# Gated linear attention followed by a multiplicative feed-forward block: loads of a step in the order alpha, k and q, v, and the logarithm tied behind the transposed copies

## The chip, the cores and the metric

The kernel runs on one core of a Trainium2 chip. The metric is the device time of one execution in microseconds (us), smaller is better. Three timed runs of the kernel before the change took 478.72, 480.35 and 480.21 us; their median is 480.21 us.

## The reference

Inputs are `q`, `k`, `v` and `alpha`, each of shape batch 4, heads 8, sequence 768, head dimension 48 in fp32, and four weight matrices of the second block in float64. The first block is a recurrence with a decay per key channel, the second a feed-forward block with a product of two projections:

```
for t in range(768):                         # per batch and head
    state = alpha[t][:, None] * state + outer(k[t], v[t])      # 48 x 48
    y[t] = q[t] @ state
x = y, heads side by side                    # 3072 tokens x 384
a, b = x @ w1, x @ w2                        # 384 -> 1024 each
out = ((a * b) @ w3) @ w_out                 # 1024 -> 1024 -> 384
```

## The kernel before, in words

**Two parts.** Part 1 runs the recurrence in chunks of 128 positions. There are 6 chunks per batch, so N = 24 chunks, numbered 0 to 23 through all batches, and it is one loop over steps n = 0 to 24 that is written out at build time. Beside the attention, part 1 converts the float64 weights `w1` and `w2` into split fp32 ([...]`to_fp32` rebuilds each number from the two words of `raw`) and, from step 6 on, fills in products of the second block (`gate`, whose matrix products all stand on the helper line L420). Part 2 does the rest of the products, folds `w3` with `w_out`, and projects.

**One chunk through part 1.** For chunk m: `load_a`, `load_kq` and `load_v` (L132, L138 and L139, L144) bring alpha, k, q and v, each 192 KB in runs of 192 bytes. `logs(m)` takes the logarithm of alpha on ScalarE (L271, called Ln(m) below), for chunks from 10 on it also splits it into two parts (L275 on ScalarE, L276 on VectorE), and for some even chunks GpSimd copies one row of alpha out to DRAM (L278). `decays(m)` sums the logarithms along the chunk on TensorE (L286 for chunks before 10, L289 from 10 on), and ScalarE takes two exponentials (L292, L293). `decayed(m)` multiplies k and q with them on VectorE (L302). `transposed(m)` transposes the result on TensorE (L324), and ScalarE copies it out of PSUM in two instructions (L326); the second copy is `mark["qkT", m]`. `scores(m)` multiplies k and q (L364) and masks on VectorE (L367); `attend_state` (L384) and `attend` (L390, copied by L394) give y; `outer` (L336) advances the state.

**What a step calls.** Step n calls, in this order of the source: the stores of y of step n-1 (L261), the load of a group of x if one is due, `load_v(n + 3)`, `load_a(n + 5)`, `load_kq(n + 4)`, `attend_state(n - 1)`, `scores(n)`, `transposed(n + 1)`, some weight conversion, `attend(n - 1)`, `outer(n)`, a product of the conversion (`third`, L232 to L234), fill pieces, `decayed(n + 2)`, `logs(n + 4)`, and `decays(n + 3)`. So alpha of a chunk is first needed one step after the step that loads it, k and q two steps after, and v three steps after. Weight conversion issues its own loads (`raw`, L192, 512 KB each) on the same queue.

**What orders the work.** All these loads are issued by SyncE (SP) in one queue. The order in which each engine and queue gets its instructions is fixed when the program is built: the Tile framework goes by the order of the source as a priority and by its own estimate of when each operand is there, and puts an instruction with a late operand behind others that come later in the source. `issue_after(ins)` (used through `after_marks`) adds an edge to that ordering: what the block traces on the engine of `ins` is placed behind `ins` on that engine. Work of the block on other engines gets no such edge.

**Buffers.** `ac` (alpha) and `kq` have three buffers, v has five, `raw` four, `la` two, `la2` one. A load into `ac` waits for the logarithm of the chunk three before and for its row copy, a load into `kq` for L302 of the chunk three before, a load into v for L390 of the chunk five before.

Of the kernel before, what the change touches and what calls it, by code (L numbers as in the profile page):

```python
# [48 lines left out]
def kernel(  # L49
# [18 lines left out]
    N = B * NCH  # L68
# [8 lines left out]
    AHEAD = 4  # L77
# [30 lines left out]
    def after_marks(*names):  # L108
        stack = ExitStack()
        for x in names:  # L110
            stack.enter_context(tc.issue_after(mark[x]))
        return stack
# [12 lines left out]
    def rows(src, n):  # L125
        b, c = divmod(n, NCH)
        return src[b, :, ds(c * C, C), :].rearrange("h p d -> p h d")

    def load_a(n):
        if n < N:  # L130
            st["a", n] = inp.tile([C, H, D], FP32, tag="ac", name="ac")
            nc.sync.dma_start(out=st["a", n], in_=rows(alpha, n))  # L132

    def load_kq(n):
        if n >= N:
            return
        st["kq", n] = inp.tile([C, 2, H, D], FP32, tag="kq", name="kq")
        nc.sync.dma_start(out=st["kq", n][:, 0], in_=rows(k, n))  # L138
        nc.sync.dma_start(out=st["kq", n][:, 1], in_=rows(q, n))  # L139

    def load_v(n):
        if n < N:
            st["v", n] = vs[n % len(vs)]
            nc.sync.dma_start(out=st["v", n][:, :, 0:D], in_=rows(v, n))  # L144
# [91 lines left out]
    def fetch(ahead=3):  # L236
        while weights and len(begun) < ahead:
            begun.append(weights.popleft())
            next(begun[-1])

    def convert(steps, ahead=3):

        for _ in range(steps):
            fetch(ahead)
            if not begun:
                return
            x = begun.popleft()
            try:
                next(x)
                begun.appendleft(x)  # L250
            except StopIteration:
                pass
# [4 lines left out]
    def store():  # L257

        while later:
            dst, src = later.popleft()  # L260
            nc.sync.dma_start(out=dst, in_=src)  # L261
# [4 lines left out]
    def logs(n):  # L266
        if n >= N:
            return
        a = st.pop(("a", n)).rearrange("p h d -> p (h d)")
        la = st["la", n] = work.tile([C, DM], FP32, tag="la", name="la")  # L270
        nc.scalar.activation(la, a, AF.Ln)  # L271
        if n >= LATE:

            t = st["la", n] = work.tile([C, 2, DM], FP32R, tag="la2", name="la2", bufs=1)
            nc.scalar.copy(t[:, 0], la)  # L275
            nc.vector.tensor_sub(t[:, 1], la, t[:, 0].bitcast(FP32))  # L276
        if n in ends:
            nc.gpsimd.dma_start(out=ends[n][2:3], in_=a[0:1])  # L278

    def decays(n):  # L280
        if n >= N:
            return
        lc = bank()[:, 0:DM]
        la = st.pop(("la", n))
        if n < LATE:
            nc.tensor.matmul(lc, sums[:, n % 2].bitcast(FP32), la, start=True, stop=True)  # L286
        else:
            for i in range(2):
                nc.tensor.matmul(lc, sums[:, n % 2], la[:, i], start=(i == 0), stop=(i == 1))  # L289

        e = st["e", n] = work.tile([C, 2, DM], FP32, tag="e", name="e", bufs=3)
        nc.scalar.activation(e[:, 0], lc, AF.Exp, scale=-1.0)  # L292
        mark["e", n] = nc.scalar.activation(e[:, 1], lc, AF.Exp).ins  # L293
        if n in ends:
            nc.gpsimd.dma_start(out=ends[n][0:1], in_=e[0:1, 0])
        if n + 1 in ends:
            nc.gpsimd.dma_start(out=ends[n + 1][1:2], in_=e[C - 1:C, 1])
        load_ends(n)

    def decayed(n):  # L300
        if n < N:
            mark["qk", n] = nc.vector.tensor_mul(qks[n % 3][:, :, :, 0:D], st.pop(("kq", n)),  # L302
                                 st.pop(("e", n)).rearrange("p i (h d) -> p i h d", h=H)).ins
# [9 lines left out]
    def transposed(n):  # L313
        if n >= N:
            return
        qk = qks[n % 3]
        qkT = work.tile([C, 2, NP, C], FP32, tag="qkT", name="qkT")

        tp = [bank().rearrange("p (i j c) -> p i j c", i=2, j=NP) for _ in range(2)]
        for i in range(2):  # L320
            for j in range(NP):
                for half in range(2):
                    s = ds(DP * half, DP)
                    nc.tensor.transpose(tp[half][:, i, j, :], qk[s, i, 2 * j:2 * j + 2, :], ident[s, s])  # L324
        for half in range(2):
            mark["qkT", n] = nc.scalar.copy(qkT[:, :, :, ds(DP * half, DP)], tp[half]).ins  # L326
        st["qkT", n] = qkT
# [30 lines left out]
    def scores(n):  # L358
        qkT = st["qkT", n]
        sc = [bank().rearrange("p (j c) -> p j c", j=NP) for _ in range(2)]  # L360
        for j in range(NP):
            for i in range(2):
                r = ds(DP * i, D)
                nc.tensor.matmul(sc[i][:, j, :], qkT[r, 0, j, :], qkT[r, 1, j, :], start=True, stop=True)  # L364
        ms = work.tile([C, 2, NP, C], FP32, tag="ms", name="ms")
        for i in range(2):
            masked = nc.vector.tensor_tensor(ms[:, i].bitcast(I32), sc[i].bitcast(I32), keep_bc, op=ALU.bitwise_and)  # L367
        ends_of_part1[0] = mark["ms", n] = masked.ins
        st["ms", n] = ms
# [3 lines left out]
    def attend_state(n):  # L373
        qkT = st.pop(("qkT", n))

        y = [bank()[:, 0:HP * C].rearrange("p (j c) -> p j c", c=C) for _ in range(2)]
        st["y", n] = y, [(half * HP + j, i, y[i][ds(DP * half, DP), j, :])
                         for j in range(HP) for i in range(2) for half in range(2)]  # L380
        if n % NCH:
            for j, i, to in st["y", n][1]:
                r = ds(DP * i, D)
                nc.tensor.matmul(to, Ts[n % 2][r, j, :], qkT[r, 1, j, :],  # L384
                                 start=(j % HP == 0), stop=False, skip_group_check=True)
# [18 lines left out]
    def load_x(g, queue=nc.sync):  # L404
        st["xT", g] = xp.tile([C, KM, TG], FP32, tag="xT", name="xT")
        queue.dma_start(out=st["xT", g], in_=xd[g].rearrange("(k p) t -> p k t", p=C))
# [82 lines left out]
    def gate(g, f):  # L489
        yield from (late_gate if late else early_gate)(g, f)  # L490
# [93 lines left out]
        logs(1)  # L584
    decays(1)
    fetch(1)
    load_v(1)
    load_kq(2)
    load_a(3)
    decayed(1)  # L590
    load_v(2)
    load_kq(3)
    load_a(4)


    begin = {4 + 4 * g: (g, range(FH if g < 4 else KF)) for g in range(5)}
# [2 lines left out]
    for n in range(N + 1):  # L599
        store()  # L600
        if n in loads:
            load_x(loads[n])
        load_v(n + AHEAD - 1)
        load_a(n + 5)
        load_kq(n + AHEAD)
        if n:
            attend_state(n - 1)
        if n < N:
            scores(n)
        transposed(n + 1)  # L610
        if n - 2 in begin:
            g, tiles = begin[n - 2]
            with after_marks(("ms", n), ("qkT", n + 1)):
                split_x(g, 0)
            fill.extend(gate(g, f) for f in tiles)
        pieces = (0, 3, 3, 2)[(n - 6) % 4] if n > 5 else 0
        if n == 0:
            with after_marks(("qkT", 0)):
                logs(2)
            decays(2)  # L620
            with after_marks(("e", 2)):
                logs(3)
        early, ready = n < 7, len(thirds)
        behind = after_marks(*[("qkT", n + 1)] * (n < N - 1), *[("qk", n + 1)] * early, *["x3"] * (n - 2 in begin))
        if n < N - 2:
            with behind:
                convert(2 if n == 0 else 1, 2 if n == 0 else 3 if n < 8 else 4)
        advance(n)
        if n:
            attend(n - 1)  # L630
        outer(n)
        third(ready)
        run(pieces > 0)
        if early:
            with after_marks(("qkT", n + 1), ("qk", n + 1)):
                convert(1)
        with after_marks(*[("ms", n)] * (n < 3)):
            decayed(n + 2)
        logs(n + 4)
        if n == 4:  # L640
            load_x(0)
        convert(early and n > 2)
        run(pieces > 1)
        decays(n + 3)
        if n < N - 2:
            convert(early or n % 3 == 0, 3 if n < 8 else 4)
        run(pieces > 2)
        if n == N - 3:
            while begun:
                convert(1)  # L650
            weights.extend(load_out(j) for j in range(KF))
            fetch(4)
# [91 lines left out]
```

## Time and profile before

| what | value |
|---|---|
| timed runs | 478.72, 480.35, 480.21 us, median 480.21 |
| profiled execution, its own time | 478.61 us |
| its span from first to last instruction | 476.8 us, so 1.8 us lie around it |
| TensorE matmul busy | 458.3 us of the span |
| TensorE busy from 64 to 187 us (rest of part 1) | 121.57 of 123.00 us |
| ScalarE busy in the same stretch | 81.30 of 123.00 us |
| mean granted TensorE clock | 0.982 |
| loads of alpha, k, q, v: median from issue to landing | 4.7, 5.4, 4.4, 5.0 us |
| instructions | 10002 |

The span is the time to which a sum over the trace is made; the median of the runs is 1.6 us above the profiled execution's own time. PE stands for TensorE's matmuls and PEld for its weight loads, ACT for ScalarE, DVE for VectorE, POOL for GpSimd, SP for SyncE. In the timeline the first number of a row is the start in us from the span's start and the second the length; what stands in brackets is how long the engine had been idle before it and what ended that. Several instructions of one line may be merged in a row (x16). PEclk is the share of full clock that TensorE was granted.

### The profile page before, as it was taken

How to read it: one execution, taken by the hardware profiler on the slowest of the kernel's cores; microseconds unless marked ns; L12 is line 12 of the kernel's file. 1: busy time of each engine (PE TensorE's matmuls, PEld its weight loads, DVE VectorE, ACT ScalarE, POOL GpSimd, SP SyncE). 2: the span in 40 equal slices, each digit the busy share in tenths (PEclk: the TensorE clock that was granted, in tenths of full speed). 3: DMA queues.
4: the chain of work that ended last, by engine and by line, in shares of the span. 5: the costliest groups of instructions: out<-in, count | busy, mean ns of one | idle time of the engine just before them, and what ended most of it. 6: DMA issues, size and time to landing. Idle time of an engine off the chain costs nothing.

```text
span 476.8 us, 10002 instructions
## 1 busy us (share of the span) xinstructions
PE 458.3 (96%) x3836; PEld 435.2 (91%) x3836; DVE 356.3 (75%) x576; ACT 282.1 (59%) x556; POOL 73.1 (15%) x140
## 2 busy tenths in 40 slices
PE   4879899999999999999999999999999999999996
PEld 2658589899899999999999999999999999999996
DVE  2769888886988988999998888745642876666761
ACT  4667766866758555898876666644545433333330
POOL 3321231112302310212331101202010100000000
PEclk9888889999999999999999999999999999999999
DMA  9999999999999964657775333122105965555511
GB/s 171 178 200 220 241 211 212 229 234 211 197 216 206 210 202 133 200 170 234 242 216 209 109 124 100 50 84 90 44 36 157 261 189 169 164 170 172 177 51 49
DMA packets 153583, 80.29 MB, mean 168 GB/s; under 512 B 104480, under 2 KB 145568, under 8 KB 153536
## 3 DMA queue, kind: packets, MB, share of 16 engines
q1 hardware_dynamic: 148016, 65.22, 56.8%
q0 software_dynamic: 5520, 14.43, 9.5%
q8 instruction: 30, 0.49, 0.5%
q14 instruction: 17, 0.14, 0.1%
HBM read 57.58 MB, written 22.06 MB: 167 GB/s over the span
## 4 chain that ended last, share of the span: by engine, by line
PE 87%; DMA 5%; SPq 3%; DVE 2%; ACT 1%; issue 1%; DVEq 0%; ACTq 0%
PE bank L420 70%; PE bank L364 5%; PE bank L390 4%; DMA raw<-in_moe_w_dram 4%; PE bank L384 2%; PE bank L324 2%; SPq L139 2%; PE bank L336 1%; PE bank L522 1%; PE bank L289 1%; DMA ac<-in_alpha_dram 1%; SPq L138 1%; SPq L132 1%; PE bank L286 1%; DVE ms L367 0%
## 5 line engine op out<-in xcount | busy, mean ns | idle before, releaser
L420 PE MATMUL bank<-x,w 128*128 128x384 f32 x1152 | 210.9, 337 | 0.0
L420 PEld LDWEIGHTS bank<-x,w 128*128 128x128 f32 x1152 | 200.4, 188 | 1.3 <-issue 0.7
L420 PE MATMUL bank<-w3o,ab 128*128 128x384 f32 x576 | 100.2, 336 | 0.0
L420 PEld LDWEIGHTS bank<-w3o,ab 128*128 128x128 f32 x576 | 99.9, 188 | 0.0
L445 ACT ACTIVATE bank<-bank 128x384 f32<-128x384 f32 x98 | 46.7, 477 | 43.6 <-PE bank L420 43.3
L429 ACT ACTIVATE t<-bank 128x384 f32<-128x384 f32 x62 | 30.6, 494 | 62.3 <-PE bank L420 60.1
L495 POOL DMA_DIRECT2D abd<-ab x46 | 26.9, 584 | 132.8 <-DVE ab L481 125.2
L481 DVE TENSOR_TENSOR ab<-bank,r 128x384 f32<-128x384 f32 x45 | 24.9, 552 | 23.4 <-ACT bank L445 18.6
L551 DVE TENSOR_TENSOR ab<-abl,ab 128x1024 fp32r<-128x1024 f32 x24 | 29.4, 1224 | 13.6 <-ACT ab L550 13.5
L550 ACT ACTIVATE ab<-abl 128x1024 fp32r<-128x1024 f32 x24 | 25.5, 1061 | 20.9 <-PE bank L420 19.2
L326 ACT COPY qkT<-bank 128x512 f32<-128x512 f32 x48 | 26.1, 591 | 19.0 <-PE bank L324 19.0
L367 DVE TENSOR_TENSOR ms<-bank,keep 128x512 int32<-128x512 int32 x48 | 31.4, 683 | 7.8 <-PE bank L364 7.8
L420 PE MATMUL bank<-wo,w3T 128*128 128x384 f32 x192 | 35.9, 334 | 0.0
L420 PEld LDWEIGHTS bank<-wo,w3T 128*128 128x128 f32 x192 | 33.5, 188 | 0.0
L364 PEld LDWEIGHTS bank<-qkT 48*128 48x128 f32 x384 | 25.7, 204 | 7.0 <-issue 4.2
L431 DVE SCALAR_TENSOR_TENSOR o<-bank,t 128x384 f32<-128x384 f32 x24 | 13.4, 557 | 24.0 <-issue 15.6
L364 PE MATMUL bank<-qkT 48*128 48x128 f32 x384 | 30.7, 304 | 0.4 <-ACT qkT L326 0.4
L552 DVE SCALAR_TENSOR_TENSOR ab<-ab,abl 128x1024 fp32r<-128x1024 f32 x24 | 29.2, 1217 | 0.0
L302 DVE TENSOR_TENSOR qk<-kq,e 128x768 f32<-128x768 f32 x24 | 23.0, 958 | 8.2 <-ACT e L293 8.1
L390 PE MATMUL bank<-ms,v 128*64 128x128 f32 x384 | 28.3, 293 | 0.0
L205 ACT ACTIVATE power<-power,rebias 128x512 uint32<-128x512 uint32 (+1 forms) x36 | 25.1, 701 | 4.1 <-DVE power L204 3.8
L200 ACT ACTIVATE rest<-raw 128x512 f32<-128x512 uint32 (+1 forms) x36 | 23.3, 650 | 7.1 <-DMA raw<-in_moe_w_dram 7.1
(80 smaller groups left out, 573.3 us busy)
## 6 DMA issues: line engine op xcount, KB each, us to landing
raw<-in_moe_w_dram SPq DMA_DIRECT2D x28, 512.0 KB, 5.2
abl<-abd SPq DMA_DIRECT2D x24, 512.0 KB, 4.6
abd<-ab POOLq DMA_DIRECT2D x46, 192.0 KB, 3.1
xT<-xd POOLq DMA_DIRECT2D x9, 576.0 KB, 4.5
ac<-in_alpha_dram SPq DMA_DIRECT2D x24, 192.0 KB, 4.7
kq<-in_k_dram SPq DMA_DIRECT2D x24, 192.0 KB, 5.4
kq<-in_q_dram SPq DMA_DIRECT2D x24, 192.0 KB, 4.4
v<-in_v_dram SPq DMA_DIRECT2D x24, 192.0 KB, 5.0
```

The lines of the kernel that those rows point to most:

```text
L205: nc.scalar.activation(power, power, AF.Relu, scale=2.0 ** 23, bias=rebias)
L326: mark["qkT", n] = nc.scalar.copy(qkT[:, :, :, ds(DP * half, DP)], tp[half]).ins
L364: nc.tensor.matmul(sc[i][:, j, :], qkT[r, 0, j, :], qkT[r, 1, j, :], start=True, stop=True)
L367: masked = nc.vector.tensor_tensor(ms[:, i].bitcast(I32), sc[i].bitcast(I32), keep_bc, op=ALU.bitwise_and)
L390: nc.tensor.matmul(to, vc[:, 2 * j + i, :], ms[:, i, j, :], start=(n % NCH == 0 and j % HP == 0), stop=(j % HP == HP - 1), skip_group_chec ...
L420: nc.tensor.matmul(p, w[part][i], x[part][i], start=start and part == parts[0] and i == 0, stop=stop and part == parts[-1] and i == n - 1, ...
L429: nc.scalar.activation(t, p1, AF.Copy, scale=(1.0 + 1.0 / P) * scale)
L445: nc.scalar.activation(p, p, AF.Copy, scale=1.0 + 1.0 / P)
L495: (nc.gpsimd if late else nc.sync).dma_start(out=abd[g][:, f, :], in_=ab)
L550: nc.scalar.activation(t[:, 0], ab, AF.Copy, scale=1.0 - 2.0 ** -13)
L551: nc.vector.tensor_sub(t[:, 1], ab, t[:, 0].bitcast(FP32))
L552: nc.vector.scalar_tensor_tensor(t[:, 2], t[:, 0].bitcast(FP32), -1.0 - 1.0 / P, ab, op0=ALU.mult, op1=ALU.add)
```

## The change

Only the order of the loads and one ordering edge change; no instruction that computes is added or taken away. In the preamble, the loads of the chunks that follow are issued alpha first, then k and q, then v. In every step the same order is used: `load_a(n + 5)`, `load_kq(n + 4)`, `load_v(n + 3)` (`AHEAD` is 4, so `n + AHEAD - 1` was already n + 3). And in steps 7 to 19 `logs(n + 4)` gets an edge behind the second copy of `transposed(n + 1)` on ScalarE.

```diff
     decays(1)
     fetch(1)
+    load_a(3)
+    load_kq(2)
     load_v(1)
-    load_kq(2)
-    load_a(3)
     decayed(1)
+    load_a(4)
+    load_kq(3)
     load_v(2)
-    load_kq(3)
-    load_a(4)
...
             load_x(loads[n])
-        load_v(n + AHEAD - 1)
         load_a(n + 5)
         load_kq(n + AHEAD)
+        load_v(n + 3)
...
-        logs(n + 4)
+        with after_marks(*[("qkT", n + 1)] * (6 < n < N - 4)):
+            logs(n + 4)
```

## The prediction

> **What bounds the kernel now.** I read the page first, for the engine that is busy:
>
> ```profile
> PE 458.3 (96%) x3836; PEld 435.2 (91%) x3836; DVE 356.3 (75%) x576; ACT 282.1 (59%) x556; POOL 73.1 (15%) x140
> PEclk9888889999999999999999999999999999999999
> DMA  9999999999999964657775333122105965555511
> ```
>
> TensorE is the bound of the whole, and the change gives it no less to do. So it can only gain where TensorE idles or runs at a reduced clock, and both lie in the first seven slices. The stretches of 3.41 us of the window view say where (length, PE busy, then the other engines, then clock):
>
> ```profile
> 15.57:18.98 3.41, 1.47 (x20) 0.80 (x18) 1.61 (x4) 2.28 (x5) 0.48 (x1) 1.00 1.17 197
> 18.98:22.40 3.42, 3.42 (x38) 3.30 (x40) 3.03 (x6) 2.19 (x6) 1.92 (x4) 0.50 1.34 183
> 29.20:32.64 3.44, 2.15 (x33) 1.55 (x32) 3.24 (x7) 3.24 (x7) 0.00 (x0) 1.00 1.20 213
> 53.12:56.53 3.41, 1.88 (x28) 1.14 (x24) 3.38 (x7) 3.20 (x8) 0.29 (x1) 1.00 0.92 166
> 56.53:59.95 3.42, 3.18 (x16) 2.11 (x18) 1.69 (x3) 2.20 (x5) 1.11 (x2) 0.50 1.01 334
> 66.77:70.20 3.43, 2.42 (x14) 2.10 (x13) 3.27 (x6) 2.20 (x5) 0.21 (x1) 1.00 1.06 228
> ```
>
> Each stretch with 2.15 us of work or less is followed by half clock; one with 2.42 us is not. Half clock holds at 18.98 to 22.40, 32.64 to 39.46 and 56.53 to 63.36: 17.1 us, half lost, 8.5 us, which is the 0.982 mean clock. From 64 to 187 us TensorE is idle for only 1.43 us. The TensorE timeline names the idle places:
>
> ```profile
> 18.07 0.91 PE L286 MATMUL bank<-la,sums 128*128 128x384 f32 x2 [1.94 <-ACT la L271]
> 34.55 1.11 PE L324 MATMUL bank<-ident,qk 64*128 64x64 f32 x16 [1.60 <-DVE qk L302]
> 54.33 0.67 PE L336 MATMUL bank<-v,qk 128*64 128x48 f32 x16 [0.68 <-ACT x L394]
> 56.77 1.65 PE L286 MATMUL bank<-la,sums 128*128 128x384 f32 x2 [1.10 <-ACT la L271]
> 68.59 0.45 PE L289 MATMUL bank<-la,sums 128*128 128x384 f32 x1 [1.01 <-ACT la L275]
> ```
>
> Three of the five wait for a logarithm (Ln(3), Ln(9), Ln(10)). The ScalarE timeline tells why each is late:
>
> ```profile
> 17.49 0.52 ACT L271 ACTIVATE la<-ac 128x384 f32<-128x384 f32 x1 [1.13 <-DMA ac<-in_alpha_dram]
> ...
> 52.56 0.70 ACT L200 ACTIVATE rest<-raw 128x512 f32<-128x512 uint32 x1 [1.13 <-DMA raw<-in_moe_w_dram]
> ...
> 54.45 1.09 ACT L326 COPY qkT<-bank 128x512 f32<-128x512 f32 x2
> 55.71 0.59 ACT L234 CAST w<-bank 128x512 fp32r<-128x512 f32 x1 [0.18 <-PE bank L233]
> 56.19 0.53 ACT L271 ACTIVATE la<-ac 128x384 f32<-128x384 f32 x1
> ...
> 67.48 0.52 ACT L271 ACTIVATE la<-ac 128x384 f32<-128x384 f32 x1
> ```
>
> Ln(3) waits for its data. Ln(9) stands behind the copies and L234, Ln(10) behind two L429, by the built order.
>
> [...]SP's loads land in the order of issue, 192 KB about every 1.05 us (raw 13.59, v1 14.61, k2 15.61, q2 16.32, alpha3 17.41, v2 18.56). The queue is full, so changing places moves a landing by whole loads and shortens nothing. [...]the clock edges here are multiples of 3.41 apart[...].
>
> **The change, part by part.**
>
> *Preamble.* Before, SP issued v1 at 8.82 and alpha3 at 13.45. Alpha3 now takes v1's place: landing 14.61 instead of 17.41, 2.8 us earlier. Ln(3) is tied behind the exponentials of chunk 2, which end at 16.36, so it starts near 16.3 instead of 17.49, and L286 near 16.8 instead of 18.07: 1.3 us of the 1.94 idle go. The stretch 15.57 to 18.98 then has 1.47 + 1.3 = 2.8 us of work, above 2.42, so the half clock at 18.98 should go too, up to 1.7 us. Alpha4 comes 3.1 us and alpha5 1.3 us earlier, so the waits of Ln(4) and Ln(5), 0.50 and 1.83, shrink. But I count all this at **nothing** in the end: TensorE then meets the weight data. Raw 1 lands at 29.38 and L200 starts at 29.40; raw 3, 4 and 5 land at 37.83, 45.76, 52.48 and are used 0.08 us later. The same loads stand ahead of each raw before and after, so these instants stay, and what is gained before them is waited there. Without this cover, up to 3.0 us.
>
> *The step's loads.* Nothing is added on SP: 24 steps of the same four DMAs. Alpha, k and q each land one load, 1.05 us, earlier; v lands three later, 3.15 us. v's slack covers that: its landing is 12.1 to 23.0 us ahead of its L390, and v1, the tightest I checked for L336, 22.96 - 14.61 = 8.3 us. The stores, raw and the x loads stay in their places behind the same number of loads; POOL's row copy, DMAs and T products have the same work with alpha earlier. If a wait for alpha's buffer now stood ahead of k and q, all SP would queue behind it, but before, alpha stood ahead of k and q too.
>
> *The effect on the built order.* This is what I can't see in the trace. Ln(9) is called in step 5 and stands behind copies of step 6, so the planner took alpha9 for late. Its real landing is 55.34, one load earlier is 54.03. If the planner shifts it by a load as well, Ln(9) goes ahead of L234 or of a qkT copy (each 0.57). Then L286(9) starts by 55.7 to 56.0: 0.8 to 1.1 us of idle go. The stretch 53.12 to 56.53 rises from 1.88 to at least 2.4 us of work, which is the edge of keeping the full clock. At full clock the run L286 to L336 from 56.77 to 63.77, 7.0 us, takes what it took in later steps and at 24 us: 0.8 + 1.1 + 0.6 + 1.0 + 0.5 = 4.0. That is 3.0 more. Not all is kept: the gate products at 64.27 need x, landed at 59.25, L412 to 60.43 and L413 (1.35) to 61.8; so the start moves from 64.27 to 61.8 at best, **2.5 us**. Next L289(10), 68.59, with 1.01 idle: alpha10 lands at 63.2, plus L271, L275, L276 at 0.5 each is 64.7, so it can follow, and moved ahead of one L429 (0.49) Ln(10) gives another **0.5**. Bounds: nothing if the order doesn't move, 2.5 + 1.01 + 0.42 (two later waits on L276) = 3.9 if all of it goes. I take 3.0. The bound below nothing is the second rival.
>
> *The edge.* It acts on ScalarE alone. In the trace every Ln(n+4) of steps 7 to 19 is already a step behind: Ln(11) 73.97 against copies of chunk 8 at 61.37, Ln(12) 80.11 against 73.01, Ln(13) 87.83 against 81.91, Ln(14) 94.42 against 89.25. What queues behind it are L429 and L394. Cost nothing as long as alpha stays the later of the two.
>
> Sum: 478.6 - 3.0 = 475.6 for an execution like the profiled one; the median stands 1.6 above it, so 480.2 - 3.0 = **477.2**.
>
> **Rivals.** *Pinned* (0.35): the built order around 56 and 67 us stays, or the half clock comes anyway, and only 0 to 1.5 us go: 479.5. For it: raw and x landings don't move, and the clock's stretches lie where they happen to. Against: three of five waits are on logarithms. *ScalarE stands on alpha* (0.20, the slower side): with alpha at the head the planner puts Ln(n+4) close behind the qkT(n+1) copies, where the real alpha hasn't landed. In steps 8 to 12 the copies end at 74.1, 83.0, 90.3, 94.5, 103.9 and alpha, one load earlier, lands at 78.1, 84.7, 92.7, 99.6, 107.2: 3.2 us of standing on average. ScalarE has 41.7 us idle in 64 to 187 over 18 steps, 2.3 each, so 0.9 reach TensorE through L429: 12 us over 13 steps, about 485 if half the steps do it. It decides once Ln moves up by more than a load plus its present margin (0.2 to 3.3 us). For it: Ln(3) to Ln(6) already stood on alpha for 0.5 to 1.8 us. Against: from Ln(9) on none did. That the loads don't move is no rival: SP's order followed the source.
>
> **Numbers.** Forecast 0.45, pinned 0.35, ScalarE on alpha 0.20. What this kernel's measurement can tell from no change is about 0.5%, 2.4 us: faster 0.45, same 0.35, slower 0.20. The range, 474.0 to 483.5: the full 3.9 and as much run spread as the three runs show (1.6) below, and a third of the slow rival above; it leaves about 0.2 out.
>
> **What would show it.** Right: L286 of chunk 3 near 16.8; raw landings unchanged to 52.5; Ln(9) ahead of L234, no half clock from 56.5, gates from about 62, v never waited for. Wrong: raw landing earlier (then the preamble's gain is kept), half clock elsewhere after 64 us, or ScalarE idle before L271 on alpha in steps 7 to 19.

## The result and the profile after

The changed kernel takes 478.57 us (median of 22 timed runs, 477.59 to 480.10), the kernel before, timed between them, 479.94 us. The ratio is 0.9974, interval 0.9963 to 0.9985: about 1.25 us less, where 3.0 were forecast. (By e3 below, which is the same built program measured a second time, it may be nearer 0.6.) The profiled execution took 478.58 us with a span of 476.8 us, the span of before's profile, which was itself 1.3 us under its kernel's median here. So the two traces show where time moves, not the difference. Three executions among the experiments (569.81 us in e7 and 634.06 us in e8 at a mean granted clock of 0.76 and 0.66, and 889.05 us in e15 at 1.00) are far slower than their fellows and are left out of medians and ratios.

The page of the changed kernel, busy time of TensorE, granted clock and DMA by slices:

```profile
PE 457.0 (96%) x3836; PEld 433.0 (91%) x3836; DVE 356.8 (75%) x576; ACT 282.0 (59%) x556; POOL 73.2 (15%) x140
PEclk9978999999999999999999999999999999999999
DMA  9989999999999965657775242122105965555511
```

Less half clock (0.989 instead of 0.982), nearly the same DMA row. The window view over the same stretches as before (length, PE, PEld, DVE, ACT, POOL busy, clock, DMA share, GB/s):

```profile
15.57:18.98 3.41, 3.07 (x48) 2.36 (x47) 2.43 (x4) 2.80 (x7) 0.78 (x2) 1.00 1.35 184
18.98:22.40 3.42, 3.05 (x46) 2.23 (x41) 3.41 (x6) 2.87 (x8) 2.11 (x4) 1.00 1.41 178
...
53.12:56.53 3.41, 2.57 (x34) 1.62 (x30) 3.39 (x7) 3.37 (x9) 0.00 (x0) 1.00 0.87 165
56.53:59.95 3.42, 2.74 (x46) 2.17 (x46) 2.88 (x5) 1.75 (x4) 1.40 (x2) 1.00 0.93 312
```

The stretches from 15.57 and 53.12 have 3.07 and 2.57 us of work instead of 1.47 and 1.88, and what follows them runs at full clock. But this execution has half clock too, once and for 10.24 us, as long as the stretches of before from 18.98 and from 32.64 together. It follows a stretch with 0.98 us of work, in which TensorE waits for weight data:

```profile
26.60:30.02 3.42, 0.98 (x6) 0.19 (x4) 0.54 (x2) 0.54 (x1) 0.97 (x2) 1.00 0.98 309
30.02:40.26 10.24, 8.80 (x80) 7.27 (x80) 9.24 (x18) 8.08 (x17) 2.13 (x3) 0.50 0.96 189
```

The TensorE timeline:

```profile
16.75 0.91 PE L286 MATMUL bank<-la,sums 128*128 128x384 f32 x2 [0.34 <-ACT la L271]
30.67 1.12 PE L384 MATMUL bank<-qkT,T 48*64 48x128 f32 x12 [3.09 <-ACT qkT L326]
56.00 0.91 PE L286 MATMUL bank<-la,sums 128*128 128x384 f32 x2 [0.34 <-ACT la L271]
61.68 0.80 PE L420 MATMUL bank<-x,w 128*128 128x384 f32 x3 [0.15 <-ACT x L412]
63.08 0.79 PE L420 MATMUL bank<-x,w 128*128 128x384 f32 x3 [0.60 <-DVE x L413]
64.44 2.32 PE L420 MATMUL bank<-x,w 128*128 128x384 f32 x12 [0.57 <-DVE x L414]
66.60 0.34 PE L289 MATMUL bank<-la,sums 128*128 128x384 f32 x1
71.92 0.71 PE L324 MATMUL bank<-ident,qk 64*128 64x64 f32 x12 [0.75 <-DVE r L431]
95.12 1.14 PE L420 MATMUL bank<-x,w 128*128 128x384 f32 x5 [1.02 <-DVE ms L367]
```

The three waits for a logarithm shrink as forecast: 1.94 to 0.34, 1.10 to 0.34, 1.01 to none. Four waits appear that before did not have: 0.60, 0.57, 0.75 and 1.02 us, together 2.94. From 64 to 187 us TensorE is now busy for 120.54 us instead of 121.57. The ScalarE timeline shows where the new ones begin:

```profile
54.44 1.09 ACT L326 COPY qkT<-bank 128x512 f32<-128x512 f32 x2
55.40 0.55 ACT L271 ACTIVATE la<-ac 128x384 f32<-128x384 f32 x1
55.82 0.60 ACT L234 CAST w<-bank 128x512 fp32r<-128x512 f32 x1
...
59.49 1.07 ACT L326 COPY qkT<-bank 128x512 f32<-128x512 f32 x2 [1.67 <-PE bank L324]
60.45 1.18 ACT L412 ACTIVATE x<-xT 128x1152 fp32r<-128x1152 f32 x1
...
64.29 0.52 ACT L271 ACTIVATE la<-ac 128x384 f32<-128x384 f32 x1
```

Ln(9) now stands ahead of L234. But L412, the first part of the split of x, stands behind the two copies of chunk 8, although x landed at 59.22; before, it ran at 59.27, ahead of them. L413 and L414 on VectorE, and the gates' products on TensorE, follow it.

### The profile page after: what moved, and what is told of

It is laid out like the page before. It is cut to its first block, busy times and chain, and to the rows that moved or that the text cites. A ratio compares the mean times of both kernels' runs of the same rounds, so it can differ in the third digit from the quotient of the medians.

```text
span 476.8 us, 10004 instructions
## 1 busy us (share of the span) xinstructions
PE 457.0 (96%) x3836; PEld 433.0 (91%) x3836; DVE 356.8 (75%) x576; ACT 282.0 (59%) x556; POOL 73.2 (15%) x140
## 4 chain that ended last, share of the span: by engine, by line
PE 85%; DMA 5%; DVE 4%; SPq 2%; ACT 2%; issue 1%; DVEq 0%; ACTq 0%
PE bank L420 70%; PE bank L364 3%; PE bank L390 3%; DMA ac<-in_alpha_dram 3%; DMA raw<-in_moe_w_dram 2%; PE bank L324 2%; SPq L139 2%; PE bank L384 2%; PE bank L522 1%; PE bank L336 1%; PE bank L289 1%; DVE qk L302 1%; PE bank L286 1%; SPq L144 1%; DVE x L414 1%
## 5 line engine op out<-in xcount | busy, mean ns | idle before, releaser
L429 ACT ACTIVATE t<-bank 128x384 f32<-128x384 f32 x62 | 30.5, 492 | 64.7 <-PE bank L420 63.2
L367 DVE TENSOR_TENSOR ms<-bank,keep 128x512 int32<-128x512 int32 x48 | 31.5, 683 | 4.1 <-PE bank L364 4.1
L431 DVE SCALAR_TENSOR_TENSOR o<-bank,t 128x384 f32<-128x384 f32 x24 | 13.4, 558 | 24.1 <-issue 15.6
L390 PE MATMUL bank<-ms,v 128*64 128x128 f32 x384 | 27.1, 285 | 0.0
```

Of the source, the lines that this page charges most:

```text
L390: nc.tensor.matmul(to, vc[:, 2 * j + i, :], ms[:, i, j, :], start=(n % NCH == 0 and j % HP == 0), stop=(j % HP == HP - 1), skip_group_chec ...
L429: nc.scalar.activation(t, p1, AF.Copy, scale=(1.0 + 1.0 / P) * scale)
```

## The experiments

Each kernel but e5, which is one execution, was timed between runs of the kernel before on the same chip:

| run | median us | before, us | ratio | interval |
|---|---|---|---|---|
| changed kernel | 478.57 | 479.94 | 0.9974 | 0.9963 to 0.9985 |
| e1 preamble alone | 478.88 | 479.00 | 1.0005 | 0.9991 to 1.0019 |
| e2 steps alone | 477.99 | 479.00 | 0.9984 | 0.9970 to 0.9997 |
| e3 no edge | 478.47 | 479.00 | 0.9987 | 0.9974 to 1.0000 |
| e4 x split first | 477.85 | 479.00 | 0.9973 | 0.9962 to 0.9985 |
| e6 changed, v behind raw | 476.92 | 478.70 | 0.9960 | 0.9944 to 0.9977 |
| e7 L276 on GpSimd | 490.19 | 478.70 | 1.0245 | 1.0198 to 1.0292 |
| e8 before, v behind raw | 475.78 | 478.69 | 0.9932 | 0.9908 to 0.9957 |
| e9 e6 and e4 together | 475.67 | 478.69 | 0.9946 | 0.9926 to 0.9967 |
| e10 before, no conversion in 7 to 9 | 479.88 | 478.69 | 1.0024 | 1.0009 to 1.0039 |
| e11 changed, the same | 479.28 | 478.69 | 1.0012 | 0.9994 to 1.0031 |
| e12 as e8 | 476.24 | 479.44 | 0.9932 | 0.9906 to 0.9957 |
| e13 before, no late v loads | 475.22 | 478.97 | 0.9918 | 0.9888 to 0.9948 |
| e14 changed, the same | 477.27 | 478.97 | 0.9966 | 0.9952 to 0.9980 |
| e15 before, no early v loads | 475.76 | 478.97 | 0.9929 | 0.9905 to 0.9952 |
| e16 changed, the same | 474.49 | 478.97 | 0.9893 | 0.9859 to 0.9926 |
| e17 new order from step 7 on | 478.84 | 480.08 | 0.9963 | 0.9940 to 0.9985 |
| e18 new order up to step 6 | 479.46 | 480.08 | 0.9983 | 0.9969 to 0.9997 |

The ratios compare runs that lie beside each other, so they can differ a little from the quotient of two medians. The letters in the expectations are readings of the cause; a letter is kept while its reading stands.

### One part of the change alone

**e1**, the preamble's order in the kernel before:

```diff
     fetch(1)
+    load_a(3)
+    load_kq(2)
     load_v(1)
-    load_kq(2)
-    load_a(3)
     decayed(1)
+    load_a(4)
+    load_kq(3)
     load_v(2)
-    load_kq(3)
-    load_a(4)
```

> The preamble's new order alone; the steps keep v, alpha, k and q, and no edge. Theory A (what is kept comes from the steps' order, which moves Ln(9) ahead of L234; the preamble's gain is waited away at the weight data that lands at 29.4): ratio to before 1.000, within 0.001, the second half-clock stretch at 56 us is still there, chunk 3's L286 near 16.8 instead of 18.07. Rival B (what is kept comes from the preamble): 0.9974.

No difference: 1.0005. The trace is worth more than the time. TensorE timeline:

```profile
56.67 0.91 PE L286 MATMUL bank<-la,sums 128*128 128x384 f32 x2 [1.10 <-ACT la L271]
61.47 3.54 PE L420 MATMUL bank<-x,w 128*128 128x384 f32 x18
66.02 0.44 PE L289 MATMUL bank<-la,sums 128*128 128x384 f32 x1 [1.01 <-ACT la L275]
...
97.89 0.44 PE L289 MATMUL bank<-la,sums 128*128 128x384 f32 x1 [0.58 <-DVE la L276]
...
128.88 0.44 PE L289 MATMUL bank<-la,sums 128*128 128x384 f32 x1 [1.13 <-DVE la L276]
```

Both idle places in front of Ln(9) and Ln(10) are whole (1.10 and 1.01), and still the gates start at 61.47, not at 64.27 as in before's profile, because no half clock fell on 56 to 63 us in this execution. And this lead over before's profile, 2.8 us at 65 us, is worth nothing at the end: the execution ends 1.3 us behind before's. It is waited away from 91 to 129 us (0.54, 0.58, 0.58 and 1.13 us are the longest waits). ScalarE's timeline says for what:

```profile
79.10 0.52 ACT L271 ACTIVATE la<-ac 128x384 f32<-128x384 f32 x1 [1.46 <-DMA ac<-in_alpha_dram]
86.64 0.52 ACT L271 ACTIVATE la<-ac 128x384 f32<-128x384 f32 x1 [1.24 <-DMA ac<-in_alpha_dram]
...
110.88 0.52 ACT L271 ACTIVATE la<-ac 128x384 f32<-128x384 f32 x1 [2.07 <-DMA ac<-in_alpha_dram]
```

Five logarithms stand on alpha, 5.2 us in all. In before's profile, with TensorE 2.8 us later at 65, none did. The loads did not come earlier with TensorE's lead: alpha of chunks 11 and 12 landed as in before's profile, within 0.1 us, and alpha of chunks 13 to 20 landed 0.8 to 2.6 us later, so part of the loss is the spread of the loads themselves.

**e2**, the order in the steps alone (preamble as before, no edge):

```diff
-        load_v(n + AHEAD - 1)
         load_a(n + 5)
         load_kq(n + AHEAD)
+        load_v(n + 3)
```

> The steps' new order alone, preamble as before and no edge. Theory A: 0.9974 as the whole change, within 0.001, with the half clock at 18.98 still there and the one at 56.5 gone, Ln(9) ahead of L234. Rival B: 1.000.

0.9984, interval clear of 1: the steps' order carries the gain, though here 0.75 us only. The waits at the x split, L324 and L367 are there too (0.60, 0.57, 0.74, 1.02).

**e3**, the whole change without the edge:

```diff
-        with after_marks(*[("qkT", n + 1)] * (6 < n < N - 4)):
-            logs(n + 4)
+        logs(n + 4)
```

> The whole change without the edge of steps 7 to 19. Theory A (the edge does nothing, since each of these logarithms is put a step later anyway): 0.9974, within 0.001, and the same order on ScalarE as the changed kernel. Rival C (the edge holds back logarithms that would stand on alpha): slower than the changed kernel, by 0.3 us or more for each step where it acts, so 1.000 or above.

The instructions of every engine stand in the same order as in the changed kernel, so the edge is inert. Its 0.9987 and the 0.9974 of the changed kernel are two measurements of one program; their distance, 0.6 us, is what such a ratio can be off by. So an effect of that size, such as e2's or e18's, is barely shown, even where its interval keeps clear of 1.

### Is the lead handed back at the split of x, or on VectorE?

**e4** puts L412 of the first split back ahead of the copies of chunk 8:

```diff
-        nc.scalar.activation(t[:, 0], x, AF.Copy, scale=1.0 - 2.0 ** -13)
+        mark["x1", g] = nc.scalar.activation(t[:, 0], x, AF.Copy, scale=1.0 - 2.0 ** -13).ins
...
-        transposed(n + 1)
+        with after_marks(*[("x1", 0)] * (n == 7)):
+            transposed(n + 1)
```

> The changed kernel, and in step 7 the copies of chunk 8 (L326) are tied behind the first split of x (L412), so that L412 starts when x has landed, near 59.3, and not at 60.45. Theory A (the lead of 2.9 us that TensorE has at 63.4 is lost first at L413 and L414, which are late by L412's place, 1.2 us): the gates' waits for L413 and L414 shrink by 1.2 us, and if nothing behind them takes it, 0.995; if VectorE, full from 62 to 75 us, hands the wait on, 0.997. Rival D (the lead is lost at the loads): no change, 0.9974, with the gates waiting for a DMA.

0.9973: next to nothing over the changed kernel. The wait for L413 only falls to 0.41 us, 0.57 us are then waited for L429, and the waits for L431 (0.76) and L367 (1.02) stay.

**e7** takes L276 off VectorE:

```diff
-            nc.vector.tensor_sub(t[:, 1], la, t[:, 0].bitcast(FP32))
+            nc.gpsimd.tensor_sub(t[:, 1], la, t[:, 0].bitcast(FP32))
```

> The changed kernel with the subtraction that splits the logarithm (L276, 14 times 0.55 us) on GpSimd in place of VectorE; GpSimd is idle most of the time there. Theory F (VectorE, full from 62 to 75 us and at 94, takes TensorE's lead back): TensorE's waits on VectorE after 64 us shrink, ratio to before 0.995. Rival G (the sum of waits is set by the order on ScalarE and the PSUM banks, or GpSimd is slower than VectorE and L289 waits for it instead): 0.9975 or above, with L289 waiting for GpSimd.

1.0245, slower by 12 us. L276 took 1.01 us on GpSimd (0.55 on VectorE) and stood in GpSimd's queue; L289 waited for it 3.06 us at 79.6 and 4.74 us at 115.9. This tells nothing about VectorE's load: the remedy was worse than the ill.

**e10 and e11** relieve VectorE in another way, in both kernels: the weight conversion is left out of steps 7, 8 and 9 and done in later steps.

```diff
-        if n < N - 2:
+        if n < N - 2 and not 6 < n < 10:
             with behind:
                 convert(2 if n == 0 else 1, 2 if n == 0 else 3 if n < 8 else 4)
...
-        if n < N - 2:
+        if n < N - 2 and not 6 < n < 10:
             convert(early or n % 3 == 0, 3 if n < 8 else 4)
```

> The kernel before with the weight conversion left out of steps 7, 8 and 9 and done in later steps instead, so that VectorE has about 7 us less to do between 60 and 80 us; same computation. It is the partner of the next run. By itself: L324 at 72.4 no longer waits for L431 and the other waits between 68 and 95 us shrink; later steps have the conversion's 7 us more, in which TensorE has filler. Theory D: ratio 0.997 to 1.001.

> The changed kernel with the same relief: no weight conversion in steps 7, 8 and 9. Theory D (the 2.9 us lead at 63 us is handed back because VectorE is full from 62 to 75 us): with VectorE relieved the lead should be kept longer, so this run beats its partner (the kernel before with the same relief) by 2 us or more, ratio to the partner 0.996 or less, and the waits for L431 and L367 at 72 and 95 us are gone. Rival K (the lead is handed back by whatever is next, VectorE full or not; the sum of the removed waits is the most that can stay): 1 to 1.5 us to the partner, as without the relief, with waits on ScalarE or on other VectorE work in their place.

The ratio of the medians of e11 and e10 is 0.9987 (0.9958 to 1.0000), 0.6 us. Of the waits for L431 and L367 at 72 and 95 us only 0.17 us is left, as expected (one of 1.61 us for L394 at 154.9 is new), but the difference did not grow to 2 us: VectorE's load was where the lead was seen to be waited for, not why it was lost. Theory D falls in this part. What e10's trace adds is a second execution in the order of before without half clock at 56 us: gates at 61.49, with 1.10 us idle before L286(9). In e11 they start at 61.17, so the changed order leads by 0.3 us there, not by 2.6 as in the first pair of profiles, and then waits 0.60 and 0.58 us for the split of x.

### Was the half clock of before typical?

**e5** is one more execution of the kernel before.

> The kernel before, unchanged, profiled a second time. Theory E (the half clock from 56.5 us in the first profile is an accident of that execution: over 75 timed runs of this kernel half clock filled 8.2 us on average, not 17.1, and each us of it cost 0.04 us): no half clock between 56 and 63 us, gates starting near 62 already, the waits for Ln(9) and Ln(10) of about 1.1 and 1.0 us still there, and a span within 1.5 us of the first. Theory A as predicted (the half clock there is the rule and costs 2.5 us): half clock from about 56.5 again and gates at 64.

479.6 us, and the half clock fell on 33.83 to 40.66 and 57.72 to 64.55: here it did come again, so this execution spoke for the forecast. The timed runs, which list a clock each, decide. Over 219 runs of the kernel before, the mean clock is 0.9914. With all of the loss taken as half clock, as the profiles show it (0.50), I estimate (1 - 0.9914) x 2 x 477 = 8.2 us of it per run, against 17.1 in the profile that the forecast was made from. The 22 runs of the changed kernel (mean clock 0.9896) have 9.9. And within a session a run's time goes up by 0.06 us (standard error 0.016) per us of half clock, wherever it lies; the forecast charged 3.0 us for 6.83, 0.44 per us.

The traces also show what stood ahead of it at 56 us. Within one execution the edges of half clock lie multiples of 3.41 us apart, within 0.02 us (3.42, 10.24, 6.82, 17.07 and 6.83 us in before's profile; 6.83, 17.06 and 6.83 in e5). Windows are here the stretches of 3.41 us counted from those edges; that the work in one window decides the clock of the next is my reading, not shown. In before's profile a window ran from 53.12 to 56.53 (1.88 us of matmuls, shown with the prediction), in e5 from 54.31 to 57.72 (1.52 us); both took in most of the idle places before L336 and L286(9), and half clock followed. In e1, counted the same way, a window ended at 55.89, in the middle of the wait for Ln(9), and the same idle time was split over two windows. The window view of e5, then of e1:

```profile
54.31:57.72 3.41, 1.52 (x22) 0.84 (x18) 3.32 (x6) 3.25 (x8) 0.80 (x2) 1.00 0.87 175
```

```profile
52.48:55.89 3.41, 2.15 (x34) 1.43 (x30) 3.38 (x7) 3.21 (x7) 0.56 (x1) 1.00 0.79 146
55.89:59.31 3.42, 2.53 (x34) 1.79 (x34) 2.82 (x5) 2.75 (x6) 0.84 (x2) 1.00 1.00 314
```

Full clock stayed in e1, and so it did in e10, e13 and e17, which have the same idle 1.10 us before Ln(9). Where the edges fall differed between two executions of one kernel: half clock began at 18.98, 32.64 and 56.53 us in before's profile, at 33.83 and 57.72 in e5. Nor is the limit that the prediction read from its profile, between 2.15 and 2.42 us, a sharp one: 2.36 us (e13, from 28.40) was followed by half clock, and 1.80 us (e11, from 152.09) and 2.15 us (e1, from 52.48) were not.

### Which loads pin the start

**e6** leaves the changed kernel as it is and moves the load of v to the end of the step, behind the step's weight data:

```diff
         load_a(n + 5)
         load_kq(n + AHEAD)
-        load_v(n + 3)
...
             convert(early or n % 3 == 0, 3 if n < 8 else 4)
+        load_v(n + 3)
```

> The changed kernel with v's load of each step behind the step's weight load, at its end. It asks whether TensorE's time up to 52 us is pinned by the landing of raw. Pinned: raw 1, 3, 4 and 5 land one load, 0.9 to 1.1 us, earlier, L200 follows each within 0.1 us, and the gates start 0.5 to 1 us earlier; if VectorE doesn't take it back later, ratio to before 0.9955, else 0.9975. Not pinned: raw lands earlier but L200 and TensorE don't follow, 0.9975 to 0.9985.

0.9960. Raw 1, 3, 4 and 5 land at 27.88, 35.63, 42.55 and 49.45 instead of 29.45, 38.14, 45.36 and 52.48, up to 3 us earlier, and no wait of over 0.2 us for the split of x is left. The time is 0.7 us under the changed kernel's by the ratios, but the two intervals overlap.

**e8** does only that, in the kernel before:

```diff
-        load_v(n + AHEAD - 1)
         load_a(n + 5)
         load_kq(n + AHEAD)
...
             convert(early or n % 3 == 0, 3 if n < 8 else 4)
+        load_v(n + 3)
```

> The kernel before with one edit: the load of v for n+3 is issued at the end of its step, behind that step's weight loads; alpha, k and q keep their places behind each other and the preamble is that of before. So raw data lands by about a load earlier per step, as in the run with v behind raw, but the step's alpha also moves up one load. Theory D (the raw landings pin steps 1 to 5; what is handed back later is handed back behind VectorE): raw 1, 3, 4, 5 land 1.5 to 3 us earlier than 29.38, 37.83, 45.76, 52.48, and most of the gain of the run with v behind raw (0.9960) is here too: ratio 0.996 to 0.998. Rival H (the gain of that run needs alpha first in the preamble): ratio 0.999 to 1.001, waits for raw gone but Ln(3) at 17.5 and the two idle places before L286 as before.

0.9932, more than expected and more than twice what the change gives, with the preamble of before and no edge. **e12** is the same kernel again, for its profile:

> Once more the kernel before with only the load of v for n+3 put at the end of its step, to have a readable profile of it and more timed runs (the one profile there was held at a granted clock of 0.66 from end to end). It differs from the changed kernel with v behind raw only in the preamble's order and in the inert edge. Theory D (raw's landing pins steps 1 to 5, the preamble's order is worth nothing): raw 1, 3, 4, 5 land as in that run, 27.9, 35.6, 42.6, 49.5 within 0.7 us, the gates' first product starts within 0.7 us of 60.9, and the ratio is 0.995 to 0.997, no different from 0.9960. Rival L (alpha and k, q first in the preamble cost time once raw no longer waits for v): raw lands earlier still by about 1 us, ratio 0.993 to 0.9945.

0.9932 again; the twelve runs of both sessions together have a median of 476.10 us. Raw 1, 3, 4, 5 land at 27.30, 35.83, 43.05, 50.56. TensorE's timeline:

```profile
54.66 0.81 PE L286 MATMUL bank<-la,sums 128*128 128x384 f32 x2
...
60.19 0.67 PE L336 MATMUL bank<-v,qk 128*64 128x48 f32 x16 [1.93 <-DMA v<-in_v_dram]
...
61.57 4.65 PE L420 MATMUL bank<-x,w 128*128 128x384 f32 x18
66.68 0.45 PE L289 MATMUL bank<-la,sums 128*128 128x384 f32 x1 [0.46 <-ACT la L275]
```

L286(9) has no idle left, and v is now the one that comes late, once, for 1.93 us. Its lead over before's profile is 2.0 us at 65 us and 1.85 us at the end, where e1, ahead by 2.8 at 65, had lost all of it: a lead that the loads share is kept. Rival L (the preamble's new order costs time here) is not shown: raw lands no earlier than in e6 on the whole, and the intervals of 0.9932 and 0.9960 overlap.

**e9** is e6 with the edit of e4.

> The changed kernel with v behind the step's weight loads and L412 of the first x split put ahead of the copies of chunk 8. It asks whether the two edits add up. Theory D: with v behind raw the waits for the x split were already at 0.14 us, so L412 earlier has nothing to take: within 0.5 us of the run with v behind raw, ratio 0.995 to 0.997. Rival: the edits add, 0.6 us more, ratio 0.9945 or less.

0.9946, 475.67 us. Between e6 and e12; the three can't be told apart. All three beat the kernel before. Against the changed kernel (0.9963 to 0.9985) only e8 and e12 are clear of its interval, and theirs is the smallest edit.

### Is the stream of loads a second bound?

**e13 and e14** leave out the loads of v for chunks 9 to 23; each of these chunks uses the v of the chunk five before it, so 15 loads of 192 KB go and all other work is the same. The order in which the engines do it is not: with other arrivals to plan for, the build put 96 of ScalarE's 556 instructions and 70 of VectorE's 576 in other places than in before, from 69 us on. **e15 and e16** do so for chunks 5 to 8.

```diff
-            nc.sync.dma_start(out=st["v", n][:, :, 0:D], in_=rows(v, n))
+            if n < 9: nc.sync.dma_start(out=st["v", n][:, :, 0:D], in_=rows(v, n))
```

> The kernel before without the loads of v for chunks 9 to 23 (each such chunk uses the v of the chunk five before, so its values are not those of the reference); all else is the same work. From step 6 on the load queue moves 192 KB less per step, about 1 us of its time. Theory M (the stream of loads is a second bound of part 1 beside TensorE, 15 loads of 1 us are a lot of slack): waits of TensorE after 64 us go, time falls by 1 to 3 us, ratio 0.994 to 0.998. Rival D (waits after 64 us come from what is queued on VectorE and ScalarE, data is there): ratio 0.999 to 1.001.

> The changed kernel without the loads of v for chunks 9 to 23 (the v of the chunk five before is used). Partner of the run before it. Theory M (the lead of 2.9 us at 63 us is lost because loads after it do not come earlier): with the later stream relieved the lead is kept, so this kernel is 2.5 us or more below its partner, ratio to the partner 0.995 or less. Rival K (the lead at 63 us over a usual execution is small, because the half clock at 56.5 was an accident of the profiled execution; what stays is the idle before Ln(10)): 0.5 to 1.5 us below the partner, ratio 0.997 to 0.999.

The kernel before gains 3.75 us (0.9918), more than the 1 to 3 expected: from 64 us on its time hangs on the loads, or on the order that the build made without them; the run can't part the two. The window view of before, and of e13, from 98 to 158 us (the last two columns are DMA share and GB/s):

```profile
98.00:158.00 60.00, 59.58 (x767) 54.88 (x770) 50.09 (x85) 43.15 (x97) 13.09 (x24) 1.00 1.03 205
```

```profile
98.00:158.00 60.00, 60.00 (x815) 55.73 (x813) 51.56 (x86) 41.94 (x96) 14.90 (x26) 1.00 0.89 206
```

TensorE is full in both, and in before the DMA engines are too (1.03): two bounds at once. Whether it is their time that binds or SyncE's queue, which in before also stood 4.9 us at loads of v (L144) between 64 and 160 us, this pair doesn't tell. But the pair went the other way than both readings had it. With the same relief the changed kernel is the slower one, by 2.05 us. TensorE's timeline of e13:

```profile
56.47 0.91 PE L286 MATMUL bank<-la,sums 128*128 128x384 f32 x2 [1.10 <-ACT la L271]
...
61.27 3.54 PE L420 MATMUL bank<-x,w 128*128 128x384 f32 x18
65.83 0.44 PE L289 MATMUL bank<-la,sums 128*128 128x384 f32 x1 [1.01 <-ACT la L275]
...
71.60 2.70 PE L420 MATMUL bank<-x,w 128*128 128x384 f32 x14
```

and of e14:

```profile
61.81 0.79 PE L420 MATMUL bank<-x,w 128*128 128x384 f32 x3 [0.15 <-ACT x L412]
63.20 0.79 PE L420 MATMUL bank<-x,w 128*128 128x384 f32 x3 [0.60 <-DVE x L413]
64.56 2.34 PE L420 MATMUL bank<-x,w 128*128 128x384 f32 x12 [0.57 <-DVE x L414]
...
72.04 0.71 PE L324 MATMUL bank<-ident,qk 64*128 64x64 f32 x12 [0.75 <-DVE r L431]
```

Neither execution had a half clock here. The order of before has its two idle places and nothing else, its L412 runs ahead of the copies:

```profile
58.48 1.17 ACT L412 ACTIVATE x<-xT 128x1152 fp32r<-128x1152 f32 x1 [0.19 <-DMA xT<-xd]
59.55 1.05 ACT L326 COPY qkT<-bank 128x512 f32<-128x512 f32 x2
```

The changed order has neither idle place but the three new waits. They are level at 49 us; at 65 us e13 leads by 2.1 us, at 75 by 2.6, and from there to the end of the trace it stays at 2.4 to 2.6. The medians are 2.05 us apart. So between 55 and 72 us the new built order is a loss, not a gain, once the accident of the half clock is out of it.

> The kernel before without the loads of v for chunks 5 to 8 (steps 2 to 5; the v of the chunk five before is used). Weight data 3, 4, 5 then come behind one, two and three loads less. Theory M (weight data pin steps 2 to 6, and this pin is what a different order of loads must beat): raw 3, 4, 5 land about 1, 2 and 3 us earlier than 37.83, 45.76, 52.48, the gates start near 61 or earlier and the time falls by 2.5 to 4 us, ratio 0.992 to 0.995, as with v behind raw. Rival D: what comes earlier is waited for behind VectorE after 62 us, ratio 0.997 to 1.000.

> The changed kernel without the loads of v for chunks 5 to 8. Partner of the run before it. The orders of the loads in steps 2 to 5 are then the same in both; only the preamble, steps 0, 1 and from 6 on, and what follows from them in the built order differ. Theory M: ratio to the partner 0.999 to 1.001, both at 0.992 to 0.995 of the kernel before. Rival K: the change still gives its 1 us, ratio to the partner 0.998 or less.

Four loads less in steps 2 to 5 give before 3.2 us (0.9929): raw 3, 4, 5 land at 37.40, 42.95 and 49.02 and the pin on the weight data is lifted, as theory M has it. e16 is 1.3 us below e15 (0.9893 against 0.9929), so the change seems to gain here too, as rival K had it; it is not shown beyond doubt, since the two intervals overlap. Its alpha of chunks 11 to 20 lands 0.8 to 2.6 us earlier than e15's.

### The two halves of the steps

**e17** has the new order in steps 7 and later only, **e18** in the preamble and steps 0 to 6 only; `n < 7` and `n > 6` choose.

```diff
+        if n < 7: load_v(n + 3)
         load_a(n + 5)
-        load_kq(n + AHEAD)
-        load_v(n + 3)
+        load_kq(n + AHEAD), load_v(n + 3) if n > 6 else None
```

> The kernel before, with the new order of loads (alpha, k and q, v) in steps 7 and later alone; preamble, steps 0 to 6 and the built order up to about 75 us are those of before, so the first x split stays ahead of the copies of chunk 8. Theory N (the change is two things after 60 us: alpha one load earlier takes away waits for alpha that hold every execution of before between 78 and 130 us, and the new built order around the first x split costs about 2 us): here only the gain is left. No wait for L413, L414 or L431 between 61 and 73 us, no wait of L289 for L276 near 98 and 129 us, time 2 to 3.5 us below before, ratio 0.993 to 0.996. Rival K (what the change gives is the idle before Ln(9) and Ln(10)): these two idles, 1.10 and 1.01 us, are still here, so ratio 0.999 to 1.001.

> The complement: the changed kernel with the order of before (v, alpha, k and q) in steps 7 and later; preamble and steps 0 to 6 as changed, so Ln(9) and Ln(10) are early and the x split is behind the copies of chunk 8. Theory N: the cost is here without the gain; waits of 0.6, 0.6 and 0.75 us for L413, L414 and L431, and ScalarE stands on alpha again between 78 and 110 us for 2 us or more; ratio 0.999 to 1.003. Rival K: the idles before Ln(9) and Ln(10) are gone, so the 1.25 us of the change are here, ratio 0.996 to 0.998.

0.9963 and 0.9983: each half seems to give something (e18's interval ends at 0.9997), and neither reading is right in full. e17 has the two idle places whole (1.10, 1.01) and no wait for L413, L414 or L431, and is still faster than before: what it gains comes after step 7, not from Ln(9) and Ln(10), against rival K. But theory N's reason for it fails: in its profile alpha of chunks 14 to 18 lands no earlier than in before's and five logarithms stand on it for 3.2 us. From 80 us on its built order, too, differs from before's, in 21 places on ScalarE and 26 on VectorE, so the gain may be that order's. e18 shows the cost as named (0.60, 0.57 and 0.48 us) and, against theory N, no logarithm standing on alpha; its L289 waits 0.75 and 0.62 us for L276. Which single waits make up the 1.25 us of the whole change is not settled; the two halves don't add up to it (0.37% and 0.17% against 0.26%), and the intervals are too wide to ask more.

## Why the prediction was right or wrong

**The loads: right up to step 7, and later on average.** Alpha 3 landed at 14.08 (14.61 forecast), Ln(3) started at 16.18, L286 at 16.75 (16.8), and the half clock at 18.98 went (10.2 us of it came from 30.02 instead). Raw 1, 3, 4 and 5 landed at 29.45, 38.14, 45.36 and 52.48, within 0.4 us of before. "Alpha, k and q each land one load, 1.05 us, earlier" can't be seen in the pair of profiles after step 7: alpha of chunks 13 to 20 landed between 0.4 us earlier and 2.0 us later than in before's. Over four traces with the new order of the steps (the changed kernel, e2, e3, e4) and three with the old one (before, e1, e5) it holds on average, with 1.6 us for chunks 9 to 23.

**The preamble counted at nothing: right.** L384 waits 3.09 us at 30.67 instead of 0.85, and e1 has no gain. e12 and e15 show that the landing of the weight data binds: in e12 raw 1, 3, 4 and 5 came 1.9 to 2.7 us earlier, in e15 raw 3, 4 and 5 by 0.4, 2.8 and 3.5 us, and each took about 3 us less (alpha came earlier in both, too).

**v has slack: right.** After the change TensorE never waited for v. e12 shows the limit: three places later still costs one wait of 1.93 us.

**The built order moves at 56 us: right in what it named.** Ln(9) went ahead of L234, L286(9) started at 56.00, the gates at 61.68 (61.8 forecast), Ln(10) earlier by 3.2 us. What I left out is that the same shift puts L412 behind the copies of chunk 8. The forecast took "the gate products need x, landed at 59.25, L412 to 60.43" over from before as fixed; L412 now ends at 61.6.

**The step that failed is the sum of 3.0 us: "At full clock the run L286 to L336 ... 3.0 more ... so the start moves from 64.27 to 61.8 at best, 2.5 us".** The profile pair shows just that, but only the idle time before Ln(9) is the change's doing. In e1, e10 and e13, with that idle time untouched, the gates start at 61.3 to 61.5, in executions in which no half clock fell on 56 us. The term was read from one execution that had 17.1 us at half clock where the mean over 219 is 8.2. The change removes none on average (9.9), and a us of half clock went with 0.06 us of time, not 0.44. The sum also took an earlier start of the gates for an earlier end of the kernel: e1's gates start 2.8 us earlier than before's, and that execution ends 1.3 us later. That half clock can lie elsewhere in the next run is what the two profiles of before show (56.53 us in one, 57.72 in the other, and 18.98 and 32.64 against 33.83). The forecast, which had one of them, took note of how far apart its edges lay and did not doubt the term.

**What stood against the rest.** 0.8 + 1.0 us of idle did go (1.10 to 0.34, 1.01 to 0). Against them stand 0.60, 0.57 and 0.75 us for the split of x and L431, and e13 against e14, both without the late loads of v, prices the exchange at 2.05 us against the change. That the whole is still 1.25 us faster comes from elsewhere; e17 puts at least part of it behind step 7. So does a comparison of the changed kernel's trace with e1's, which has the old order of the steps and no half clock at 56 us (TensorE's instructions stand in the same order in both): the changed kernel is 2.2 us behind at 75 us, 0.5 behind at 100, and 1.3 ahead from 129 us to the end. What it wins, it wins between 90 and 129 us, where e1 has the waits listed above. That is one execution each, and e1's lies 1.0 us above its median; which waits make up the gain of the medians stays open.

**The bound I did not name.** "TensorE is the bound of the whole" is true of the page's sum and not of part 1. The DMA row that I quoted holds nines for 14 of 40 slices, 167 us, and the window view shows a DMA share near 1 from 12 to 158 us:

```profile
12.00:158.00 146.00, 137.69 (x1749) 119.96 (x1751) 120.05 (x205) 103.27 (x225) 31.23 (x58) 0.94 1.04 211
```

That loads bind there is what e13 and e15 speak for: 15 loads less, 3.75 us; four loads less at the right place, 3.2 us. From 12 to 158 us TensorE and the DMA engines are both nearly full in before's profile (137.69 of 146.00 us, share 1.04), from 187 to 470 us TensorE alone is (283.00 of 283.00 us, share 0.47). In e1 a lead of TensorE that the loads didn't share was waited away (2.8 us at 65, none at the end).

**The rivals.** *Pinned* (0 to 1.5 us) is what the time says, and its first reason is half right: raw and x landings did not move, though the built order did. *ScalarE stands on alpha* did not happen: after the change two logarithms stood on it, for 0.05 and 0.96 us, and reached nobody. The edge cost nothing, as counted: without it (e3) the engines' order is the same.

## What to carry to other kernels

A stretch of half clock in one profile is a sample, not a property (17.1 us in the profile here, 8.2 on the mean of 219 runs): before it is priced, look at the clock of many runs, at whether their time follows it (0.06 us per us here), and at where half clock lay in other profiles of the kernel. Where the DMA share is near 1 beside a full TensorE (1.03 and 59.58 of 60.00 us here, from 98 to 158 us), ask of a new order of loads which transfer that pins someone lands earlier; here it was the weight data, and moving v behind them in the kernel before gave 3.2 us (e8, e12), while the change, with v behind k and q only, gave 1.25. An order that is built from estimated arrivals moves as a whole, so list what else stood near the moved instruction, and what comes to stand in front of it.

## What the runs showed of the hardware

On GpSimd the subtraction of 128x384 took 1.01 us (e7) where VectorE took 0.55 (before). In the changed kernel one issue of q (L139) held SyncE's own queue for 4.05 us from 26.56, with two loads of raw, one of alpha and one of k ahead of it still under way, the first of these until 29.45; what it waited for isn't shown. Stretches of 3.41 us with 0.98 us of matmuls (changed kernel, from 26.60), 1.47 and 1.88 (before, from 15.57 and 53.12) and 1.52 (e5, from 54.31), in which no single idle time was longer than 2.43 us, were followed by half clock; one with 1.80 (e11, from 152.09) was not.
